# Chunk attention feeding a mixture of experts on one core: softmax held in PSUM, attention of later token pairs at fixed places

## The chip, the cores and the metric

The kernel runs on one core of a Trainium2 chip. The metric is the device time in microseconds (us) of one execution; the time before is the median of three runs. Five engines work side by side, each through its own list of instructions in order: TensorE (PE) multiplies, VectorE (DVE) and ScalarE (ACT) read and write PSUM and SBUF, GpSimd (POOL) works in SBUF, and SyncE (SP) issues the DMAs.

## The reference

Inputs are q, k, v of shape 8 x 8 x 576 x 64 (batch, heads, sequence, head size), four expert probabilities for each of 4608 tokens, and two weight matrices for each of four experts.

```
scores = q_c @ k_c^T / 8            # in chunks of 64 positions, nothing across chunks
attn   = exp(scores - max(scores))
attn   = attn / (sum(attn) + 1e-9)
x      = attn @ v_c                 # then (4608 tokens, 512)
p      = probs / (sum(probs) + 1e-9)
out    = sum over e of  p[:, e] * (relu(x @ w1[e]) @ w2[e])     # 512 -> 1024 -> 512
```

## The kernel before

**Stages.** The 4608 tokens are nine blocks of 512: one block by itself, and then four pairs of blocks. Each expert's hidden size of 1024 is cut in two, so there are eight passes over weights for each stage: passes 0 to 7 for the single block (`startup`, `plain_pass`), passes 8 to 15 for pair 0 (`first_pair_pass`), and passes 16 to 39 for pairs 1, 2 and 3 (`later_pass`, eight passes each). A pair is multiplied by a scheme of seven products in place of eight, over 2 x 2 blocks of weights (a11 to a22, sums s1 to s4) and tokens or hidden values (b11 to b22, sums t1 to t4).

**Two halves of a number.** An fp32 operand is split into a rounded "hi" part, which ScalarE casts, and the remainder "lo", which VectorE or GpSimd makes by subtraction. Each product is then three matmuls (`TERMS`, L455), issued at L461.

**Units of the later passes.** In a later pass the first matrix's units are called g1 to g7 and h1 to h7 (`LaterGroup`, two halves of the rows), and the second matrix's units of the pass before are a1 to a7 and b1 to b7 (`Outer`). A unit is six matmuls. `WOVEN` is the written order of the 28 units; a "place" below is an index into it:

```
0 a1  1 g1  2 a2  3 g2  4 g6  5 a5  6 g5  7 a6  8 a3  9 g7  10 a7  11 g4  12 g3  13 a4
14 h1 15 h2 16 b1 17 b5 18 h6 19 b6 20 b3 21 h5 22 b7 23 h7 24 b2 25 b4  26 h4  27 h3
```

After the unit at each place come the functions listed in `at` for it. What g and h leave in PSUM is copied (L523), added (L662), cut at zero and scaled (L628) by ScalarE and VectorE into hidden values; their sums are at L634, their hi casts at L640 and their lo parts on GpSimd at L643. What a and b leave is added to the output sums by VectorE (L689). The banks are named: g and h use A0, B0, C0, and a and b use A1, B1, C1, so a unit waits until VectorE or ScalarE has read what the unit before left in its bank. Pass 16 has no a or b units, as no pass of this kind lies before it, and runs g and h alone in the same order.

**Attention.** A tile is 128 tokens; eight tiles make a pair. A tile has five steps (`STEPS`): scores (PE into the PSUM tile "psa" of two banks), softmax (VectorE maximum L148 and subtraction L149, ScalarE exponential L153), weights (VectorE sum L197, plus 1e-9 L202, reciprocal L203, multiplication L204), transpose (PE L163 and ScalarE L165) and values (PE L172 and ScalarE L179). The generator `attention` yields between steps, and `Beside.go` takes steps at a rate: in passes 17 to 22 of a pair (and 25 to 30 of the next) it is called at the eight places of `ASIDE` (1, 4, 8, 11, 15, 18, 22, 25), with 40 steps spread over 42 calls. The tiles of the first block have functions of their own in `startup` (L186 to L204 by way of `less_max`, `a_exp`, `a_norm`).

**Weights and the ring.** During passes 8 to 15 the split weights are written to DRAM. Later passes read them back in units of 512 KB through six SBUF buffers: three for the first matrix (ring 0) and three for the second (ring 1), refilled by `ring_next` when both halves of a unit are used. All these DMAs go through SyncE's list.

Of the kernel before, what the change touches and what calls it, by code (L numbers as in the profile page):

```python
# [30 lines left out]
def chunk_attention_moe(ctx: ExitStack, tc: tile.TileContext, qk, v, v0, dp, w1, w2, out):  # L31
# [110 lines left out]

    def a_softmax(t):

        s = st[t]
        e = s["e"] = att.tile([P, HG, 2, C], F32, name="e")
        m = small.tile([P, 2, HG], F32, name="m")
        nc.vector.tensor_reduce(out=m, in_=s["sc"], op=ALU.max, axis=AX)  # L148
        nc.vector.tensor_tensor(  # L149
            out=e.rearrange("p j c k -> p c j k"), in0=s["sc"],  # L150
            in1=m.unsqueeze(3).broadcast_to([P, 2, HG, C]), op=ALU.subtract,
        )
# [29 lines left out]

    def less_max(a, src):
        n = a.shape[1]
        m = small.tile([P, n], F32, name=f"m{n}")
        nc.vector.tensor_reduce(out=m, in_=src, op=ALU.max, axis=AX)  # L186
        nc.vector.tensor_tensor(
            out=a, in0=src, in1=m.unsqueeze(2).broadcast_to([P, n, C]), op=ALU.subtract
        )

    def a_exp(a):
        nc.scalar.activation(out=a, in_=a, func=AF.Exp, scale=1.0 / C**0.5)

    def a_norm(e):
        n = e.shape[1]
        z = small.tile([P, n], F32, name=f"z{n}")
        nc.vector.tensor_reduce(out=z, in_=e, op=ALU.add, axis=AX)  # L197
        a_scale(e, z)

    def a_scale(e, z):  # L200
        n = e.shape[1]
        nc.vector.tensor_scalar_add(z, z, 1e-9)  # L202
        nc.vector.reciprocal(out=z, in_=z)  # L203
        nc.vector.tensor_tensor(  # L204
            out=e, in0=e, in1=z.unsqueeze(2).broadcast_to([P, n, C]), op=ALU.mult
        )

# [649 lines left out]
    nc.vector.memset(zeros, 0.0)  # L857
    idle = ps_a.tile([P, SUB], F32, name="psa")

    def keep_warm(n, cols=SUB):  # L860

        for _ in range(n):
            nc.tensor.matmul(
                idle[:, :cols], lhsT=zeros[:, :P], rhs=zeros[:, :cols], start=True, stop=True
            )
# [12 lines left out]

    def start_e(t):
        return att.tile([P, 2 * HG, C], F32, name=("e", "pt")[t % 2])  # L880

    def subtract_max(t):
        es[t] = start_e(t)
        less_max(es[t], sc[t])

    def startup(beside):
# [21 lines left out]
        start_x(1)  # L908
        subtract_max(2)
        a_exp(es[2])  # L910
        w_load(1, 0, 1, 0)
# [4 lines left out]
        plain_hidden(0, first, order=RHS_LO_LAST)  # L916
        a_norm(es[2])
        w2_split(0, 1)
        plain_hidden(1, first, order=RHS_LO_LAST)
        subtract_max(3)  # L920
        a_exp(es[3])
        w2_split(1, 0)
        plain_hidden(2, first, order=RHS_LO_LAST)
        start_transpose(2)
        a_norm(es[3])
        w2_split(1, 1)
# [55 lines left out]
    def plain_pass(n, beside, x, ahead_of=None):  # L982
# [32 lines left out]
        add(at, 4, lambda: w[0].hi("a12"), lambda: x.hi("b21"), lambda: w[0].hi("s1"))  # L1015
        add(at, 4, lambda: w[0].lo("a12"), lambda: x.lo("b21"), lambda: w[0].lo("s1"))
        add(at, 5, lambda: w[0].sum3(), lambda: w[0].sum4(), ahead_of.load)
        add(at, 6, lambda: w[0].hi("s3"), lambda: w[0].lo("s3"))
        add(at, 6, lambda: w[0].hi("a22"), lambda: w[0].lo("a22"))
        add(at, 6, lambda: w[0].hi("s4"), lambda: w[0].lo("s4"))  # L1020
# [4 lines left out]
    def first_pair_pass(n, held, made, beside, ahead_of):  # L1025

# [19 lines left out]
        begin_w2 = 5 if n == n_pass else 0  # L1046
        if begin_w2 == 0:
            add(at, 0, w2.sum1, w2.sum2)
# [43 lines left out]
        add(at, 13, lambda: x.lo("t1"), lambda: x.hi("t3"))  # L1092
        add(at, 14, lambda: x.lo("t3"))
        add(at, 16, lambda: x.hi("b22"))
        add(at, 17, lambda: x.lo("b22"))
        add(at, 17, lambda: [ring_load(i, r) for r in range(3) for i in range(2)])
        add(at, 18, x.sum2, lambda: x.hi("t2"))
        add(at, 19, lambda: probs_load(n + 1, 0), lambda: probs_load(n + 1, 1))
        add(at, 19, lambda: x.lo("t2"))
        add(at, 20, x.sum4, lambda: x.hi("t4"))  # L1100
        add(at, 20, ahead_of.load)
        add(at, 21, lambda: x.lo("t4", nc.gpsimd))
        issue(steps, at, beside)
# [24 lines left out]
    def later_pass(n, ahead, late, beside, ahead_of):  # L1128

# [3 lines left out]
        left, sc = Units(n), Scaled(n)  # L1133
        steps = {f"gh"[g]: LaterGroup(g, left, sc, False) for g in range(2)}
        if ahead:
            steps |= {"ab"[g]: Outer(g, n - 1, ahead[1], ahead[0], False) for g in range(2)}

# [3 lines left out]
        for i, f in late:  # L1141
            add(at, i, f)
        if ahead:
            second_half(at, ahead[0])

# [22 lines left out]
        if last_pass and more:  # L1168
# [11 lines left out]
            late = [  # L1180
                (0, lambda: x.hi("b22")), (0, ahead_of.load),
                (7, lambda: x.lo("t4", nc.gpsimd)), (7, lambda: x.lo("b22", nc.gpsimd)),
            ]
        for i, name in enumerate(WOVEN):
            if name[0] in steps:
                getattr(steps[name[0]], f"p{name[1]}")()
# [62 lines left out]
    with tc.manual_schedule():  # L1249
        beside = [Beside(0, (n_pass - 3) * 2 * NK), Beside(1, (n_pass - 1) * 26 - 4)]  # L1250
        beside += [Beside(pair, (n_pass - 3) * len(ASIDE) + 2) for pair in range(2, n_pairs + 1)]
        startup(beside[0])
        x = None
        for n in range(1, n_pass):
            if n == n_pass - 2:
                x = Tokens(0)
            held, made = plain_pass(n, beside[0], x, beside[1] if n == n_pass - 1 else None)
        for n in range(n_pass, 2 * n_pass):
            held, made = first_pair_pass(n, held, made, beside[1], beside[2])
        ahead, late = None, []  # L1260
        for n in range(2 * n_pass, n_run):
            pair = n // n_pass - 1
            ahead, late = later_pass(
                n, ahead, late, beside[1 + pair], beside[min(2 + pair, n_pairs)]
            )
        last_products(ahead)
# [45 lines left out]
```

## Time and profile before

| | us |
|---|---|
| median of three runs (1585.38 to 1593.53) | 1587.99 |
| profiled execution | 1587.58 |
| its span, first to last instruction | 1585.8 |
| PE busy in the span | 1531.3 |
| DVE busy | 924.8 |
| POOL busy | 888.0 |
| ACT busy | 574.9 |

The profiled execution's time is 1.8 us more than its span, and 0.4 us less than the median. "Idle" before an instruction is the time in which its engine had nothing running; the name behind the arrow is what ended it, by engine, tile and line. A row of stages gives the stage's limits and length, then for each engine its busy time and its count of instructions, and then the granted TensorE clock (1.00 is full), the DMA share and GB/s.

### The profile page before, as it was taken

What the parts mean: (1) busy time and instruction counts of PE and PEld (TensorE: products, weight loads), DVE (VectorE), ACT (ScalarE), POOL (GpSimd) and SP (SyncE); (2) the same over time, 40 slices, a digit from 0 to 9 for tenths busy, and PEclk for the clock granted to TensorE, in tenths of its full rate; (3) what the DMA queues carried; (4) which work ended last, traced back from release to release, by engine and by line L of the source; (5) the groups of instructions that cost most, each with busy time, mean ns of one, the idle gap of its engine ahead of it and who ended that gap; (6) DMA issues with size and microseconds to landing.
All of it is one profiled execution on the core that took longest, in us unless ns stands there. A gap on an engine that the chain in (4) does not pass through costs nothing.

```text
span 1585.8 us, 23406 instructions
## 1 busy us (share of the span) xinstructions
PE 1531.3 (97%) x8854; PEld 1238.8 (78%) x8854; DVE 924.8 (58%) x1287; ACT 574.9 (36%) x999; POOL 888.0 (56%) x665
## 2 busy tenths in 40 slices
PE   7999999999999999999999999998999999999998
PEld 5878877888888777787777777786877788888886
DVE  5444554444444555766767855666667755566665
ACT  3343443344444424332333434232333443323332
POOL 2343576677766525545555665444455755555654
PEclk9999999999999999999999999999999999999999
DMA  5344347877666575656655667565655576666664
GB/s 188 120 124 138 107 165 251 297 249 237 231 226 225 200 249 173 212 187 209 201 194 184 196 211 236 182 226 174 203 191 191 179 232 207 194 204 195 203 193 138
DMA packets 164831, 314.16 MB, mean 198 GB/s; under 512 B 14176, under 2 KB 79984, under 8 KB 164720
## 3 DMA queue, kind: packets, MB, share of 16 engines
q1 hardware_dynamic: 164720, 312.68, 60.6%
q8 instruction: 70, 1.15, 0.3%
q14 instruction: 41, 0.34, 0.1%
HBM read 244.39 MB, written 68.23 MB: 197 GB/s over the span
## 4 chain that ended last, share of the span: by engine, by line
PE 80%; DVE 9%; POOL 5%; ACT 2%; DMA 1%; issue 1%; SPq 0%; DVEq 0%; ACTq 0%; POOLq 0%
PE A L461 39%; PE C L461 23%; PE B L461 14%; POOL hfl L643 2%; DVE acc L689 1%; DVE wraw L634 1%; PE psa L172 1%; DVE e L204 1%; PE psa L138 1%; PE psa L163 1%; DVE z L202 1%; POOL wf L279 1%; DVE xl L279 1%; POOL hfl L279 1%; DVE z L197 1%
## 5 line engine op out<-in xcount | busy, mean ns | idle before, releaser
L643 POOL TENSOR_TENSOR hfl<-wraw,hfh 128x512 fp32r<-128x512 f32 x288 | 388.1, 1367 | 219.7 <-ACT hfh L640 196.5
L461 PE MATMUL A<-xh,wf 128*128 128x512 f32 (+1 forms) x1112 | 384.8, 392 | 11.2 <-DVE wraw L628 9.5
L461 PE MATMUL A<-hfh,wf 128*128 128x512 f32 x768 | 272.2, 396 | 10.2 <-DVE acc L689 10.2
L461 PEld LDWEIGHTS A<-xh,wf 128*128 128x128 f32 x1112 | 207.9, 188 | 59.4 <-DVE wraw L628 12.2
L523 ACT COPY s<-A 128x512 f32<-128x512 f32 x192 | 112.6, 587 | 385.7 <-PE A L461 385.1
L640 ACT CAST hfh<-wraw 128x512 fp32r<-128x512 f32 x288 | 172.3, 622 | 203.7 <-POOL wraw L634 61.0
L461 PE MATMUL A<-xl,wf 128*128 128x512 f32 (+1 forms) x556 | 215.2, 388 | 0.0
L461 PE MATMUL C<-xh,wf 128*128 128x512 f32 (+1 forms) x584 | 201.0, 391 | 1.7 <-DVE B L662 1.7
L461 PEld LDWEIGHTS A<-hfh,wf 128*128 128x128 f32 x768 | 145.1, 189 | 44.0 <-DVE acc L689 13.4
L689 DVE TENSOR_TENSOR acc<-A,acc 128x512 f32<-128x512 f32 x174 | 119.4, 686 | 99.7 <-PE A L461 99.4
L461 PE MATMUL A<-hfl,wf 128*128 128x512 f32 x384 | 150.7, 393 | 0.0
L461 PE MATMUL C<-hfh,wf 128*128 128x512 f32 x384 | 134.7, 392 | 0.2
L279 POOL TENSOR_TENSOR hfl<-wraw,hfh 128x512 fp32r<-128x512 f32 x64 | 87.2, 1388 | 84.0 <-ACT hfh L276 79.0
L634 POOL TENSOR_TENSOR wf<-wraw,wf 128x512 f32<-128x512 f32 x24 | 31.1, 1296 | 177.6 <-DVE wf L628 177.6
L461 PEld LDWEIGHTS C<-xh,wf 128*128 128x128 f32 x584 | 109.2, 188 | 24.9 <-DVE B L662 2.2
L461 PE MATMUL B<-xh,wf 128*128 128x512 f32 (+1 forms) x384 | 126.9, 384 | 1.3 <-DVE acc L757 1.3
L279 POOL TENSOR_TENSOR wf<-wraw,wf 128x512 fp32r<-128x512 f32 x70 | 93.5, 1358 | 56.8 <-ACT wf L276 56.6
L461 PEld LDWEIGHTS A<-xl,wf 128*128 128x128 f32 x556 | 104.4, 188 | 20.4 <-POOL xl L279 0.6
L461 PE MATMUL C<-xl,wf 128*128 128x512 f32 (+1 forms) x292 | 113.0, 389 | 1.4 <-POOL xl L279 1.4
L689 DVE TENSOR_TENSOR acc<-C,acc 128x512 f32<-128x512 f32 x90 | 62.0, 689 | 66.3 <-PE C L461 65.7
L643 POOL TENSOR_TENSOR hfl<-wf,hfh 128x512 fp32r<-128x512 f32 x48 | 72.6, 1512 | 44.1 <-ACT hfh L640 43.8
L461 PEld LDWEIGHTS C<-hfh,wf 128*128 128x128 f32 x384 | 72.1, 188 | 16.2 <-DVE acc L689 1.1
(177 smaller groups left out, 2738.2 us busy)
## 6 DMA issues: line engine op xcount, KB each, us to landing
wf<-w SPq DMA_DIRECT2D x336, 512.0 KB, 4.0
wraw<-in_w SPq DMA_DIRECT2D x128, 256.0 KB, 3.7
w<-wf SPq DMA_DIRECT2D x112, 256.0 KB, 4.3
qk_in<-in_qk SPq DMA_DIRECT2D x32, 512.0 KB, 4.5
v_in<-in_v SPq DMA_DIRECT2D x32, 256.0 KB, 4.0
w<-hfl SPq DMA_DIRECT2D x32, 256.0 KB, 2.4
w<-hfh SPq DMA_DIRECT2D x32, 256.0 KB, 2.6
w<-hfh SPq DMA_DIRECT2D x48, 128.0 KB, 2.7
```

Of the source, the lines that this page charges most:

```text
L138: nc.tensor.matmul(s["sc"][half, c, j], lhsT=s["x"][rows, g, 0, h], rhs=s["x"][rows, g, 1, h], start=True, stop=True,)
L163: nc.tensor.transpose(ps[:, j], s["e"][:, j].rearrange("p c k -> p (c k)"), ident)
L172: nc.tensor.matmul(av[half, c, j], lhsT=s["v"][rows, 2 * j + odd], rhs=s["pt"][rows, j, half], start=True, stop=True,)
L197: nc.vector.tensor_reduce(out=z, in_=e, op=ALU.add, axis=AX)
L202: nc.vector.tensor_scalar_add(z, z, 1e-9)
L279: eng.tensor_tensor(out=t[1], in0=src, in1=t[0].bitcast(F32), op=ALU.subtract)
L461: nc.tensor.matmul(out, lhsT=lhs(k, a), rhs=rhs(k, b), start=first and i == 0, stop=last and i == len(parts) - 1, skip_group_check=not (fi ...
L523: nc.scalar.copy(out=t, in_=self.a)
L634: (eng or nc.vector).tensor_tensor(out=self.values[place, k], in0=self.values[a, k], in1=self.values[b, k], op=op)
L640: nc.scalar.copy(out=self.part(name, 0)[:, k], in_=self.values[name, k])
L643: (eng or nc.gpsimd).tensor_tensor(out=self.part(name, 1)[:, k], in0=self.values[name, k], in1=self.part(name, 0)[:, k].bitcast(F32), op=A ...
L689: nc.vector.tensor_tensor(out=acc[key], in0=src, in1=acc[key], op=ALU.add)
```

## The change

- **Softmax.** Maximum, subtraction and exponential now work in place in PSUM; the sum of the exponentials and its addition of 1e-9 lie in an unused part of the same PSUM tile (in `startup`, of the tile that keeps PE warm, which becomes two banks). The reciprocal goes to SBUF, and the last multiplication reads PSUM and writes the weights `e` to SBUF. `e` is allocated at the weights step, not at the softmax step; "psa" is held until then.
- **Startup order.** The weights of tile 0 come ahead of the softmax of tile 1.
- **Attention of pairs 2 and 3.** In later passes the rate is gone. `TILES` says which tile is worked on in which pass, at the places `EARLY` (4, 6, 9, 11) or `LATE` (13, 17, 21, 24): scores, softmax and the next loads at the first place, weights at the second, transpose at the third, values at the fourth.
- **Pass 16** has a function and an order of its own, in which g and h are mixed and have separate banks (A0, B0, C0 and A1, B1, C1); its ring loads are at first all for ring 0.
- **First tiles of pair 1.** In pass 15 the hi and lo parts of the tokens come later, one pair of them at a place; in passes 7 and 8 the parts of the weight blocks a22, s3 and s4 change place.
- **In later passes** the sum t4 of the first half goes on GpSimd behind b21's lo part, one place later.

```diff
     def a_scores(t):
         s = st[t]
-        s["sc"] = halves(ps_a.tile([P, 2, 2 * HG * C], F32, name="psa"))
+        s["psa"] = ps_a.tile([P, 2, 2 * HG * C], F32, name="psa")
+        s["sc"] = halves(s["psa"])
...
     def a_softmax(t):
+        less_max(st[t]["sc"])
+        a_exp(st[t]["sc"])
+
+    def a_weights(t):
         s = st[t]
-        e = s["e"] = att.tile([P, HG, 2, C], F32, name="e")
-        m = small.tile([P, 2, HG], F32, name="m")
-        nc.vector.tensor_reduce(out=m, in_=s["sc"], op=ALU.max, axis=AX)
-        nc.vector.tensor_tensor(
-            out=e.rearrange("p j c k -> p c j k"), in0=s["sc"],
-            in1=m.unsqueeze(3).broadcast_to([P, 2, HG, C]), op=ALU.subtract,
-        )
-        nc.scalar.activation(out=e, in_=e, func=AF.Exp, scale=1.0 / C**0.5)
-
-    def a_weights(t):
-        e = st[t]["e"].rearrange("p j c k -> p (j c) k")
-        a_norm(e)
+        s["e"] = att.tile([P, HG, 2, C], F32, name="e")
+        z = s["psa"][:, 0, HG * C : HG * C + 2 * HG].rearrange("p (c j) -> p c j", c=2)
+        a_norm(s["e"].rearrange("p j c k -> p c j k"), s["sc"], z)
...
+    def less_max(a):
+        m = small.tile(a.shape[:-1], F32, name=f"m{len(a.shape)}")
+        nc.vector.tensor_reduce(out=m, in_=a, op=ALU.max, axis=AX)
+        m = m.unsqueeze(len(a.shape) - 1).broadcast_to(a.shape)
+        nc.vector.tensor_tensor(out=a, in0=a, in1=m, op=ALU.subtract)
...
+    def a_norm(e, a, z):
+        nc.vector.tensor_reduce(out=z, in_=a, op=ALU.add, axis=AX)
         nc.vector.tensor_scalar_add(z, z, 1e-9)
+        r = small.tile(a.shape[:-1], F32, name=f"z{len(a.shape)}")
+        nc.vector.reciprocal(out=r, in_=z)
+        r = r.unsqueeze(len(a.shape) - 1).broadcast_to(a.shape)
+        nc.vector.tensor_tensor(out=e, in0=a, in1=r, op=ALU.mult)
...
     def ring_next(i, r):
         last = n_ring - N_SLOT
-        if r + 3 < n_ring and (i == 0 or r < last):
+        if i == 0 and 3 <= r < 6:
+            ring_load(1, r - 3)
+        elif i == 0 and r < 3:
+            ring_load(0, r + 6)
+        elif i == 0 and r + 3 < n_ring or r < last:
             ring_load(i, r + 3)
...
     def startup(beside):
...
-        subtract_max(0)
-        a_exp(es[0])
-        subtract_max(1)
-        a_exp(es[1])
+        start_softmax(0)
+        start_weights(0)
+        start_softmax(1)
         for f, k in QUADS[:3]:
             w1_split(f, k, nc.gpsimd)
-        a_norm(es[0])
         start_transpose(0)
         w1_split(1, 1, nc.gpsimd)
-        a_norm(es[1])
+        start_weights(1)
...
-        add(at, 8, lambda: x.hi("b11"))
-        add(at, 9, lambda: x.lo("b11"), lambda: x.hi("b21"))
-        add(at, 10, lambda: x.lo("b21"))
-        add(at, 12, lambda: x.hi("t1"))
...
-        add(at, 17, lambda: [ring_load(i, r) for r in range(3) for i in range(2)])
...
+        for i, name in zip((13, 14, 16, 17, 19), ("b11", "b21", "t1", "t3", "b22")):
+            add(at, i - 1, lambda name=name: x.hi(name))
+            add(at, i, lambda name=name: x.lo(name))
+        add(at, 17, lambda: [ring_load(0, r, (RINGS[0] + RINGS[1])[r]) for r in range(6)])
...
-    ASIDE = (1, 4, 8, 11, 15, 18, 22, 25)
+    EARLY, LATE = (4, 6, 9, 11), (13, 17, 21, 24)
+    TILES = {
+        1: ((LATE, 0),), 2: ((EARLY, 1),), 3: ((EARLY, 2), (LATE, 3)), 4: ((EARLY, 4),),
+        5: ((EARLY, 5), (LATE, 6)), 6: ((EARLY, 7),),
+    }
...
+    def attend(at, pair, places, i):
+        t = (1 + pair * PAIR) * NT + i
+        add(at, places[0], lambda: a_scores(t), lambda: a_softmax(t), lambda: a_load_v(t))
+        if i + 1 < PAIR * NT:
+            add(at, places[0], lambda: a_load(t + 1))
+        for place, step in zip(places[1:], STEPS[2:]):
+            add(at, place, lambda step=step: step(t))
+
+    FIRST = "g1 g2 g6 g5 h1 g7 h2 h6 g4 g3 h5 h7 h4 h3".split()
+
+    def first_later_pass(n, *_):
+        at = {}
+        left, sc = Units(n), Scaled(n)
+        steps = {"gh"[g]: LaterGroup(g, left, sc, True) for g in range(2)}
...
+        for i, name in enumerate(FIRST):
+            getattr(steps[name[0]], f"p{name[1]}")()
+            for f in at.get(i, ()):
+                f()
+        return (sc, left), []
...
     def later_pass(n, ahead, late):
...
-        add(at, 25, lambda: sc.sum("t4", 0, nc.gpsimd))
         put(26, "b21", 1)
+        add(at, 26, lambda: sc.sum("t4", 0, nc.gpsimd))
...
+        if pair + 1 < n_pairs:
+            for places, i in TILES.get(n % n_pass, ()):
+                attend(at, pair + 1, places, i)
...
-            if i in ASIDE and not first_pass and not last_pass and (n % n_pass > 1 or i > 16):
-                beside.go()
```

More of the change, by code (lines that the diff above doesn't have):

```diff
@@ L857, in chunk_attention_moe @@
     nc.vector.memset(zeros, 0.0)
-    idle = ps_a.tile([P, SUB], F32, name="psa")
+    idle = ps_a.tile([P, 2, SUB], F32, name="psa")
     def keep_warm(n, cols=SUB):
@@ L863, in keep_warm @@
             nc.tensor.matmul(
-                idle[:, :cols], lhsT=zeros[:, :P], rhs=zeros[:, :cols], start=True, stop=True
+                idle[:, 0, :cols], lhsT=zeros[:, :P], rhs=zeros[:, :cols], start=True, stop=True
             )
@@ L877, in load_all, with start_softmax, start_weights @@
         w_load(1, 0, 0, 1)
[L879 to L884, printed above, removed]
+    def start_softmax(t):
+        less_max(sc[t])
+        a_exp(sc[t])
+    def start_weights(t):
+        es[t] = att.tile([P, 2 * HG, C], F32, name=("e", "pt")[t % 2])
+        a_norm(es[t], sc[t], idle[:, 1, t * 2 * HG : (t + 1) * 2 * HG])
     def startup(beside):
@@ L1023, in plain_pass, with first_pair_pass @@
         return steps[-1], w[0]
-    def first_pair_pass(n, held, made, beside, ahead_of):
+    def first_pair_pass(n, held, made, beside):
         last_pass = n % n_pass == n_pass - 1
@@ L1046, in first_pair_pass @@
         begin_w2 = 5 if n == n_pass else 0
[L1047 removed]
+        if begin_w2:
+            for name in ("s3", "s4"):
+                add(at, 0, lambda name=name: made.hi(name), lambda name=name: made.lo(name))
+        else:
             add(at, 0, w2.sum1, w2.sum2)
@@ L1124, in chunk_attention_moe, with first_load, put, later_pass @@
     )
-    ASIDE = (1, 4, 8, 11, 15, 18, 22, 25)
-    ALONE = "a1 b1 a2 a5 b5 a6 b6 a3 b3 a7 b7 b2 a4 b4".split()
-    def later_pass(n, ahead, late, beside, ahead_of):
+    EARLY, LATE = (4, 6, 9, 11), (13, 17, 21, 24)
[3 more added lines that the diff above has]
+    }
+    ALONE = "a1 b1 a2 a5 b5 a6 b6 a3 b3 a7 b7 b2 a4 b4".split()
+    def first_load(pair):
+        if pair < n_pairs:
+            a_load((1 + pair * PAIR) * NT)
+    def attend(at, pair, places, i):
[10 more added lines that the diff above has]
+        steps = {"gh"[g]: LaterGroup(g, left, sc, True) for g in range(2)}
+        def put(i, name, k):
+            add(at, i, lambda: sc.hi(name, k), lambda: sc.lo(name, k))
+        put(2, "b11", 0)
+        put(6, "b22", 0)
+        put(7, "b11", 1)
+        put(9, "b21", 0)
+        add(at, 9, lambda: sc.sum("t3", 0), lambda: sc.sum("t2", 0))
+        put(10, "t2", 0)
+        add(at, 11, lambda: sc.sum("t1", 0))
+        put(12, "b22", 1)
+        put(12, "t1", 0)
+        add(at, 12, lambda: sc.sum("t4", 0, nc.gpsimd))
+        put(13, "b21", 1)
+        put(13, "t3", 0)
+        add(at, 13, lambda: sc.sum("t1", 1), lambda: sc.sum("t3", 1))
+        for i, name in enumerate(FIRST):
[3 more added lines that the diff above has]
+        return (sc, left), []
+    def later_pass(n, ahead, late):
         first_pass, last_pass = n % n_pass == 0, n % n_pass == n_pass - 1
@@ L1133, in later_pass @@
         left, sc = Units(n), Scaled(n)
-        steps = {f"gh"[g]: LaterGroup(g, left, sc, False) for g in range(2)}
-        if ahead:
-            steps |= {"ab"[g]: Outer(g, n - 1, ahead[1], ahead[0], False) for g in range(2)}
+        steps = {"gh"[g]: LaterGroup(g, left, sc, False) for g in range(2)}
+        steps |= {"ab"[g]: Outer(g, n - 1, ahead[1], ahead[0], False) for g in range(2)}
         def put(i, name, k, of=sc):
@@ L1258, in chunk_attention_moe @@
         for n in range(n_pass, 2 * n_pass):
-            held, made = first_pair_pass(n, held, made, beside[1], beside[2])
+            held, made = first_pair_pass(n, held, made, beside[1])
         ahead, late = None, []
         for n in range(2 * n_pass, n_run):
[L1262 to L1265, printed above, removed]
+            ahead, late = (later_pass if n > 2 * n_pass else first_later_pass)(n, ahead, late)
         last_products(ahead)
```

55 lines of the change are left out of this document (13 added, 42 removed).

## The prediction

> **What bounds the kernel.** First the page's head (the profiled execution took 1587.58 us, 1.8 more than its span), then the span cut by stages, to see where PE has nothing to run. The stage rows give limits, length, then PE, PEld, DVE, ACT and POOL busy time with counts, granted clock, DMA share, GB/s.
>
> ```profile
> span 1585.8 us, 23406 instructions
> ```
>
> ```profile
> 0.00:34.00 34.00, 23.57 (x311) 17.97 (x312) 20.02 (x36) 13.04 (x24) 11.54 (x14) 0.97 0.67 219
> 222.00:573.00 351.00, 346.70 (x1989) 281.59 (x1990) 166.45 (x235) 146.89 (x259) 230.58 (x180) 1.00 0.74 250
> 573.00:605.00 32.00, 26.76 (x113) 20.51 (x112) 17.94 (x22) 11.41 (x20) 17.12 (x13) 1.00 0.39 129
> 605.00:880.00 275.00, 263.52 (x1616) 212.18 (x1615) 179.62 (x255) 89.21 (x155) 142.96 (x108) 0.99 0.62 200
> 880.00:920.00 40.00, 37.67 (x160) 29.13 (x159) 30.74 (x39) 18.30 (x28) 31.01 (x19) 1.00 0.61 193
> 950.00:1225.00 275.00, 263.51 (x1621) 212.17 (x1620) 178.21 (x254) 90.67 (x158) 141.45 (x107) 0.99 0.62 202
> 1225.00:1265.00 40.00, 37.67 (x160) 29.15 (x159) 30.98 (x39) 18.30 (x28) 31.25 (x19) 1.00 0.58 186
> 1265.00:1560.00 295.00, 295.00 (x1319) 244.19 (x1317) 176.27 (x245) 98.63 (x170) 171.38 (x131) 1.00 0.64 203
> ```
>
> PE is the bound: in 1265 to 1560, passes with no attention, it is never idle, and 295 us over 1319 matmuls are 0.224 us each, so a unit of six takes 1.34. The change removes no PE work, so all it can win is PE idle time. The two stretches with attention of pairs 2 and 3 lose 275.00 - 263.52 = 11.48 and 11.49 us. Pass 16 (573 to 605) loses 5.24, the two pair changes (880 to 920, 1225 to 1265) 2.33 each, passes 8 to 15 lose 4.30.
>
> Next, who ends the idle time in 605 to 880 (total, times, longest), and the clock just after two of its stalls:
>
> ```profile
> PE A L461 <- DVE wraw L628: 4.7, 2, 2.4
> PE A L461 <- DVE acc L689: 4.6, 2, 2.3
> PE psa L163 <- DVE e L204: 2.2, 2, 1.2
> 673.80:677.20 3.40, 3.40 (x10) 2.72 (x11) 1.15 (x2) 0.38 (x1) 0.45 (x1) 0.50 0.00 0
> 1107.30:1110.70 3.40, 3.40 (x11) 2.71 (x11) 1.32 (x3) 0.62 (x1) 0.28 (x2) 0.50 0.00 0
> ```
>
> All of it is VectorE arriving late, in six stalls per pair. After two of the eight long ones (over both pairs) the granted clock is 0.50 for 3.4 us, which costs another 1.7 us of PE work each.
>
> One of each long kind, in the timeline (start, length, instruction, idle before it):
>
> ```profile
> 725.90 0.68 DVE L197 TENSOR_REDUCE z<-e 128x8 f32<-128x512 f32 x1
> 726.61 1.14 DVE L202 TENSOR_SCALAR z<-z 128x8 f32<-128x8 f32 x1
> 728.02 1.47 DVE L204 TENSOR_TENSOR e<-e,z 128x512 f32<-128x512 f32 x1
> 729.41 0.68 DVE L628 SCALAR_TENSOR_TENSOR wraw<-A,s 128x512 f32<-128x512 f32 x1
> 730.15 0.50 PE L461 MATMUL A<-xh,wf 128*128 128x512 f32 x1 [2.39 <-DVE wraw L628]
> ```
>
> The weights of a tile were issued at place 25, between b4 and h4. VectorE spends 725.90 to 729.41 on them and only then reads h4's bank A0, for which the next pass's g1 waits 2.39 us.
>
> ```profile
> 666.76 1.13 ACT L640 CAST hfh<-wraw 128x512 fp32r<-128x512 f32 x2
> 667.44 2.54 POOL L643 TENSOR_TENSOR hfl<-wraw,hfh 128x512 fp32r<-128x512 f32 x2 [5.28 <-DVE acc L689]
> 668.77 1.76 DVE L634 TENSOR_TENSOR wraw<-wf,wraw 128x512 f32<-128x512 f32 x1 [1.39 <-POOL hfl L643]
> 673.05 0.68 DVE L689 TENSOR_TENSOR acc<-A,acc 128x512 f32<-128x512 f32 x1
> 673.78 0.80 PE L461 MATMUL A<-hfh,wf 128*128 128x512 f32 x1 [2.29 <-DVE acc L689]
> ```
>
> Here the softmax had been issued at place 15. Its exponential stood in ScalarE's list ahead of b11's casts (666.76), GpSimd's lo parts came late, the sum t2 (668.77) waited 1.39 us for them, the weights at place 18 stood behind that sum, and b6's output addition (673.05) behind the weights. Unit b7 (673.78) needs b6's bank. The third kind is a transpose issued too soon after its weights.
>
> **The change, part by part.** *Softmax in PSUM.* The rows of its instructions (minimum/median/maximum ns):
>
> ```profile
> L204 DVE TENSOR_TENSOR e<-e,z x34: 691/1476/1709, 11.8 to 1190.0; 128x512 f32<-128x512 f32 x34
> L202 DVE TENSOR_SCALAR z<-z x36: 171/468/1276, 11.4 to 1188.5; 128x8 f32<-128x8 f32 x36
> L149 DVE TENSOR_TENSOR e<-psa,m x32: 691/691/694, 53.7 to 1182.3; 128x512 f32<-128x512 f32 x32
> L148 DVE TENSOR_REDUCE m<-psa x32: 680/681/686, 53.0 to 1181.6; 128x8 f32<-128x512 f32 x32
> L197 DVE TENSOR_REDUCE z<-e x34: 674/676/679, 10.7 to 1187.8; 128x8 f32<-128x512 f32 x34
> ```
>
> The multiplication with both operands in SBUF takes 1476 in the median; the subtraction of the same shape, with its large operand in PSUM, never over 694. The new multiplication is of that second form, so I take 0.69 (ends 0.69 and 1.48). The addition on z moves to PSUM, where no row shows it: between 0.17 and 0.47, and I take 0.2, as its long cases look like the multiplication's. The reciprocal keeps some 0.2, what the timeline leaves between 727.75 and 728.02. Weights then cost 0.68 + 0.2 + 0.2 + 0.69 = 1.8 us against 0.68 + 0.47 + 0.2 + 1.48 = 2.8 in the median. That alone gives PE nothing; it shortens the stalls. Maximum and subtraction stay, and the exponential only changes its memory, hidden beside matmuls. "psa" is held longer, but its next user is the same tile's transpose, which waits for the weights anyway.
>
> [...]
>
> *Fixed places.* Weights come at place 6 or 17 and never behind b4, so the 2.4 us stalls at g1 go. The late softmax is at 13, and its weights at 17 come ahead of t2 (place 18), not behind it; the exponential no longer stands before b11's casts. Transposes follow weights by three or four units, 4.0 us or more, against 1.8 us of work. What is late next? For an early tile, the weights can begin about 2.2 us after the scores (0.68 + 0.69 + the exponential's 0.63 and the hand-overs), and two units last 2.7; behind them waits a6's addition, whose bank is wanted three units later: nothing lost. For a late tile, b5's addition ends near 667.4 in the example, the weights 669.2, t2 by 669.9 to 671.0, b6's addition by 670.6 to 671.7, and PE would be ready for b7 at 671.3: 0 to 0.4 us lost, for six late tiles 0 to 2.4. I take 1.0. Gain: 11.48 + 11.49 + 2 x 1.7 - 1.0 = **25.4 us**.
>
> *Pass 16.* The waits in 573 to 605:
>
> ```profile
> PE B L461 <- POOL hfl L643: 2.0, 1, 2.0
> PE C L461 <- DVE B L662: 1.7, 1, 1.7
> PE A L461 <- ACT s L523: 1.5, 2, 0.7
> ```
>
> Mixing g and h removes the copy wait between g7 and g4. But h6's copy goes to the tile "s2" that g3's addition, two units later, still has to read; ScalarE stands until then, casts and the copy of h7 queue behind it, and VectorE's sums for t2 with them. I work this out as about 0.2 at h7, 1.9 at h4, and 1.1 at pass 17's a2, whose last lo part is fourth in GpSimd's list: 3.2 against 5.24. Gain **2.0** (0 to 5.2). The six first ring loads are the same number of bytes; nothing waits for them before.
>
> *First tiles reordered.* In passes 8 to 15 the largest stall stands behind these:
>
> ```profile
> PE C L461 <- DVE hfl L469: 2.4, 4, 1.6
> 544.89 2.33 DVE L279 TENSOR_TENSOR xl<-xraw,xh 128x1024 fp32r<-128x1024 f32 x1
> 547.74 1.71 DVE L279 TENSOR_TENSOR xl<-xraw,xh 128x1024 fp32r<-128x1024 f32 x1
> ```
>
> The two lo parts of b11 and b21 sit between g3's result and the reading of its bank. They move four places later, behind that reading. Gain **1.6** (0 to 2.4). They are hidden behind the four whole output tiles (12 matmuls, 2.7 us each) that end pass 15; without these the last one, t4's, would be late by its own length, about 2.3 us. The moves in passes 7 and 8 I put at nothing, hidden behind matmuls; the 2.7 us left in this stage bound them.
>
> *t4 behind b21.* At each pair change GpSimd is busy 31 of 40 us, so its b21 part comes one operation earlier, but its later parts end when they did. Gain **1.0** of the 4.66 (0 to 1.9).
>
> *Startup.*
>
> ```profile
> 10.79 0.63 ACT L192 ACTIVATE pt<-pt 128x512 f32<-128x512 f32 x1 [1.88 <-DVE pt L187]
> 11.33 1.64 ACT L276 CAST wf<-wraw 128x512 fp32r<-128x512 f32 x3
> 13.33 0.59 ACT L836 COPY s<-B 128x512 f32<-128x512 f32 x1 [0.36 <-PE B L832]
> 29.23 1.15 PE L845 MATMUL A<-s,ws 64*64 64x64 f32 x32 [1.45 <-ACT s L836]
> 31.34 0.69 DVE L204 TENSOR_TENSOR pt<-pt,z 128x512 f32<-128x512 f32 x1
> ```
>
> Tile 1's maximum and subtraction now stand behind tile 0's weights, so its exponential (10.79) slips by about 1.6, the three casts with it, and the copy of tile 0's transpose (13.33) to 14.6: 1.25 us late, into the first hidden product. The cheaper weights win most of it back (tile 3's end at 31.4 in place of 32.0). But tile 2's values (29.23) go to the bank where tile 3's scores lie, now held until tile 3's weights end, so their 1.15 us move behind it. Loss **0.8** (-0.6 to 1.6).
>
> Sum: -25.4 - 2.0 - 1.6 - 1.0 + 0.8 = -29.2 us, so 1587.58 - 29.2 = 1558.4 for the profiled execution. That one stood 0.4 below the median of 1587.99; I forecast **1558.5**.
>
> **Rivals.** *Half of it stays.* If the b7 stalls come from GpSimd's lateness and not from the order, the four of 2.3 us and the two half-clock stretches stay: 9.2 + 3.4 = 12.6, time 1571. For it: the 1.39 us wait in the row at 668.77. Against it: 1265 to 1560 has the same sums and no idle.
>
> *The idle time only changes place.* If PE is ahead of VectorE or GpSimd by as much at the new places, the 23 us come back: about 1584. Against it: VectorE is busy 179.62 of 275 us there, POOL 142.96; neither is full.
>
> *Slower.* At place 4 or 13 the exponential is issued only one or two units before other ScalarE work and its weights two units later. If ScalarE stands at the exponential long enough that each of the 16 tiles meets one 2.3 us stall (a6's or b6's addition late), that is 36.8 us plus the clock halved for one in four, 4 x 1.7 = 6.8, against 30.2 saved: 1601. It decides from 1.9 us per tile on. The slack reckoned above speaks against it.
>
> *More than that.* Pass 16, the pair changes and startup at their good ends, no late-tile loss: 25.4 + 1.0 + 5.2 + 2.4 + 1.9 + 0.6 = 36.5, so 1551.
>
> **How the numbers follow.** Forecast 0.62, with its own range 1553 to 1565 from the ends of the small terms; half stays 0.20; changes place 0.07; slower 0.06; more 0.05. The range 1550 to 1575 holds the first two and the last, 0.87. What can be told from no change here is 0.5%, 8 us: faster 0.87, same 0.07, slower 0.06.
>
> **What would show it.** Right: between 605 and 1225 no PE wait on L628 or L689 over 0.5 us, no clock of 0.50 there, the final multiplication near 0.69 in all tiles; no wait at 550; pass 16 still losing about 3 us, at h4 and at a2. Wrong: new waits of about 2 us at a7, b7 or a transpose once per tile, or startup's first output product more than 1.6 us late.

## The result, and the profile after

The changed kernel takes **1561.48 us** in the median of four runs (1560.53 to 1562.57), against 1588.52 for the kernel before (the three runs behind 1587.99 and a fourth, 1585.38 to 1593.53): a ratio of 0.9827, 95% interval 0.98 to 0.9854. Its profiled execution took 1560.53 us. Its page's head:

```profile
span 1558.7 us, 23407 instructions
PE 1527.6 (98%) x8854; PEld 1240.8 (80%) x8854; DVE 918.0 (59%) x1288; ACT 574.3 (37%) x999; POOL 883.2 (57%) x664
```

The span is 27.1 us shorter, with the same 8854 matmuls. Where this came from can be read from the first matmul of a pass, since PE does the same work between two of them. PE's timeline, at the first matmul of pass 8, 16, 24, 32 and of the last products; first the kernel before, then after:

```profile
219.60 0.47 PE L461 MATMUL A<-xh,wf 128*128 128x512 f32 x1
573.36 0.39 PE L461 MATMUL A<-xh,wf 128*128 128x512 f32 x1
899.55 0.50 PE L461 MATMUL A<-hfh,wf 128*128 128x512 f32 x1 [0.53 <-DVE acc L689]
1244.79 0.50 PE L461 MATMUL A<-hfh,wf 128*128 128x512 f32 x1 [0.53 <-DVE acc L689]
1556.15 0.39 PE L461 MATMUL A<-hfh,wf 128*128 128x512 f32 x1
```

```profile
222.69 0.47 PE L455 MATMUL A<-xh,wf 128*128 128x512 f32 x1
574.52 0.39 PE L455 MATMUL A<-xh,wf 128*128 128x512 f32 x1
885.17 0.50 PE L455 MATMUL A<-hfh,wf 128*128 128x512 f32 x1 [0.53 <-DVE acc L683]
1217.16 0.50 PE L455 MATMUL A<-hfh,wf 128*128 128x512 f32 x1 [0.48 <-DVE acc L683]
1528.57 0.39 PE L455 MATMUL A<-hfh,wf 128*128 128x512 f32 x1
```

| stretch | before | after | moved by | forecast |
|---|---|---|---|---|
| start to pass 8 | 219.60 | 222.69 | +3.09 | +0.8 |
| passes 8 to 15 | 353.76 | 351.83 | -1.93 | -1.6 |
| passes 16 to 23 | 326.19 | 310.65 | -15.54 | -14.7 |
| passes 24 to 31 | 345.24 | 331.99 | -13.25 | -13.2 |
| passes 32 to 39 | 311.36 | 311.41 | +0.05 | -0.5 |
| rest of the span | 29.65 | 30.13 | +0.48 | 0 |

The forecast for passes 16 to 23 is half of the 25.4 us for the fixed places, and 2.0 for pass 16; for 24 to 31 the other half, and half of t4's 1.0. The sum of the moves is -27.1, that of the forecast -29.2.

The stages of the changed kernel, in the columns of the rows before (limits, length, PE, PEld, DVE, ACT, POOL, clock, DMA share, GB/s):

```profile
576.00:608.00 32.00, 29.94 (x124) 23.96 (x123) 19.24 (x23) 13.02 (x23) 19.33 (x14) 0.95 0.52 164
608.00:850.00 242.00, 242.00 (x1535) 196.61 (x1534) 164.18 (x236) 84.74 (x147) 131.00 (x101) 1.00 0.65 209
850.00:906.00 56.00, 51.85 (x222) 40.77 (x221) 44.32 (x57) 21.26 (x33) 40.20 (x24) 1.00 0.61 201
940.00:1182.00 242.00, 242.00 (x1539) 196.71 (x1538) 163.84 (x236) 85.67 (x149) 129.65 (x99) 1.00 0.66 211
1182.00:1238.00 56.00, 52.19 (x223) 40.98 (x222) 44.32 (x57) 21.23 (x33) 40.13 (x24) 1.00 0.61 193
```

In 608 to 850 and 940 to 1182, where the attention of pairs 2 and 3 runs, PE is never idle: all twelve stalls are gone, and no clock of 0.50 is left there. But 850 to 906 and its twin 1182 to 1238 lose 4.15 and 3.81 us, where the kernel before loses 2.33 at the pair change. The waits of the kernel before in 880 to 920, and of the changed kernel in 850 to 906:

```profile
PE B L461 <- POOL hfl L643: 0.9, 1, 0.9
PE C L461 <- POOL xl L279: 0.7, 1, 0.7
PE A L461 <- DVE acc L689: 0.5, 1, 0.5
```

```profile
PE C L455 <- DVE acc L683: 1.6, 1, 1.6
PE A L455 <- POOL xl L268: 1.2, 1, 1.2
PE C L455 <- POOL xl L268: 0.7, 1, 0.7
PE A L455 <- DVE acc L683: 0.5, 1, 0.5
```

The first two of the changed kernel are new. The wait of 1.6 is at a3 of pass 23, the last pass of the pair, that of 1.2 at g4 of pass 24, and both have their like at the next pair change (1.3 and 1.1). The wait of 0.9 before, at a2 of pass 24, is gone.

The softmax's instructions (ns, minimum/median/maximum) came out as taken:

```profile
L195 DVE TENSOR_TENSOR e<-psa,z x32: 690/691/692, 61.3 to 1147.0; 128x512 f32<-128x512 f32 x32
L191 DVE TENSOR_SCALAR psa<-psa x36: 173/174/175, 11.9 to 1146.6; 128x8 f32<-128x8 f32 x36
```

The addition's 174 ns in PSUM stand beside a least of 171 in SBUF, and the sum's 690 from PSUM (median) beside 676 from SBUF: 3 and 14 ns more.

### The profile page after: what moved, and what is told of

Same layout as the page of the kernel before. It is cut to its first block, busy times and chain, and to the rows that moved or that the text cites. A ratio compares the mean times of both kernels' runs of the same rounds, so it can differ in the third digit from the quotient of the medians.

```text
span 1558.7 us, 23407 instructions
## 1 busy us (share of the span) xinstructions
PE 1527.6 (98%) x8854; PEld 1240.8 (80%) x8854; DVE 918.0 (59%) x1288; ACT 574.3 (37%) x999; POOL 883.2 (57%) x664
## 4 chain that ended last, share of the span: by engine, by line
PE 87%; DVE 4%; POOL 4%; DMA 3%; ACT 2%; issue 1%; SPq 0%; DVEq 0%; ACTq 0%; POOLq 0%
PE A L455 42%; PE C L455 25%; PE B L455 15%; PE psa L168 1%; PE psa L139 1%; POOL hfl L637 1%; PE psa L159 1%; DVE xl L268 1%; DMA w<-hfh 1%; DMA w<-wf 1%; POOL wf L268 1%; DMA wraw<-in_w 1%; DVE acc L683 1%; POOL xl L268 1%; PE psa L769 1%
## 5 line engine op out<-in xcount | busy, mean ns | idle before, releaser
L683 DVE TENSOR_TENSOR acc<-A,acc 128x512 f32<-128x512 f32 x174 | 119.3, 685 | 79.6 <-PE A L455 78.6
L683 DVE TENSOR_TENSOR acc<-C,acc 128x512 f32<-128x512 f32 x90 | 62.0, 690 | 58.9 <-PE C L455 54.6
```

Source lines behind the costliest of these rows:

```text
L683: nc.vector.tensor_tensor(out=acc[key], in0=src, in1=acc[key], op=ALU.add)
```

## The experiments

All are edits of one of the two kernels; in the diffs "..." marks what is left out. Where a pass is said to begin at a time, that is its first matmul in PE's timeline. Traces of the same code differ by one or two us among themselves (startup of the kernel before: the first output product at 32.85 and, in the run of softmax alone, at 33.86; the changed kernel: pass 16 at 574.52 and, timed again, at 575.58). A stretch of half clock (1.6 us in pass 16 below) or a single wait (1.2 us at g1 of pass 24) comes in some of them and not in others. So a time from one run is weak evidence below that.

**Softmax in PSUM alone, and fixed places alone.** The first takes the kernel before and gives only the tiles of pairs 0 to 3 their new softmax. The second takes the changed kernel, with all its other parts, and gives these tiles their old softmax.

```diff
# psum_only: the kernel before
     def a_softmax(t):
+        in_place_max(st[t]["sc"])
+        a_exp(st[t]["sc"])
+
+    def a_weights(t):
...
-        e = s["e"] = att.tile([P, HG, 2, C], F32, name="e")
...
+        psum_norm(s["e"].rearrange("p j c k -> p c j k"), s["sc"], z)
# places_only: the changed kernel, the same exchange the other way round
```

`in_place_max` and `psum_norm` are what the changed kernel calls `less_max` and `a_norm`.

> The kernel before, with only the softmax of the tiles of pairs 0 to 3 kept in PSUM; startup, the rate of the attention steps, pass 16 and the first tiles are as before. Theory (the order in VectorE's list makes the stalls, their length is set by the weights): the multiplication falls to 0.69 us and the addition to 0.2, so the four stalls at g1 (2.39) lose about 1.75 each, the four at b7 (2.29) about 0.8, the four at the transpose nearly all; some 9 of the 23 us stay and the clock is not halved there: about 1571. Rival (only the places matter): 20 us or more of the 23 stay, about 1584.

> The changed kernel, but with the softmax of the tiles of pairs 0 to 3 in SBUF as before (startup's tiles stay in PSUM). Theory: at the new places the 2.8 us of weights have room too, at most 0.8 us more is lost at b7 for each of six late tiles: 1561 to 1566. Rival (the fixed places only work because the weights are short): a stall of 1 us or more for each of 14 tiles in pairs 2 and 3, above 1573.

Measured: softmax alone 1571.09 us (ratio to the kernel before 0.9897, interval 0.9873 to 0.992); places alone 1561.64 (0.984, 0.9822 to 0.9858). The waits of softmax alone in 605 to 880, and of places alone its stages with attention:

```profile
PE A L471 <- DVE acc L699: 3.0, 2, 1.5
PE A L471 <- DVE wraw L638: 1.3, 2, 0.6
```

```profile
608.00:850.00 242.00, 242.00 (x1535) 196.74 (x1535) 164.49 (x235) 85.01 (x148) 132.10 (x101) 1.00 0.66 210
942.00:1184.00 242.00, 242.00 (x1539) 196.78 (x1538) 165.59 (x236) 85.99 (x149) 130.53 (x99) 1.00 0.67 211
```

With softmax alone the stalls at b7 and g1 keep their places and lose what VectorE saves in them, 2.3 to 1.5 and 2.4 to 0.6; those at the transpose go, and the clock behind the eight that stay is 1.00. With the places alone every one of them is gone, although the multiplication takes up to 1.82 us again. So the two parts are two ways to the same gain and do not add: either the weights get short, or they get a place where their length does not matter. The second reaches further: on top of it the short weights show no gain, 0.984 against the changed kernel's 0.9827. Both rivals fall.

**Late tiles' weights at place 25.** The place of the old stall at g1, with the short weights.

```diff
-    EARLY, LATE = (4, 6, 9, 11), (13, 17, 21, 24)
+    EARLY, LATE = (4, 6, 9, 11), (13, 25, 26, 27)
```

> The changed kernel with LATE = (13, 25, 26, 27): the weights of six tiles come at place 25, between b4 and h4, as in the stall of the kernel before. Theory: h4's bank is read 1.8 us late, so g1 waits 0.5 to 0.8 us (2.39 less the 1.75 that PSUM saves), and the transpose at 26 waits about 0.7 for its weights: 1.0 to 1.6 us a tile, 6 to 10 us in all, about 1569. Rival (with short weights the place does not matter): under 1 us in all, 1561 to 1562.

Measured: 1567.76 us in one run. The waits in 605 to 880:

```profile
PE psa L159 <- DVE e L195: 3.2, 3, 1.3
```

Beside these only the 1.6 at a3 is left, which the changed kernel has too. The place matters: 6 us in all, as the theory said. But of the two waits it added up, only one is there. The transposes at 26 take all of it (0.5 to 1.3 each), and g1 does not wait. It would not wait without them either: at the tile with the longest wait, VectorE has read h4's bank at 720.82, and g1 comes at 724.43. With softmax alone the weights at place 25 begin 0.9 us after h4 ends (725.67), here 0.7 before it ends (718.36). The softmax now stands at 13, no longer a few places ahead of the weights; that this is the reason was not tested.

**t4 back at place 25.** In the changed kernel GpSimd's sum t4 comes behind b21's lo part.

```diff
+        add(at, 25, lambda: sc.sum("t4", 0, nc.gpsimd))
         put(26, "b21", 1)
-        add(at, 26, lambda: sc.sum("t4", 0, nc.gpsimd))
```

> The changed kernel with the GpSimd sum t4 back at place 25, ahead of b21's lo part. Theory: the waits that the changed kernel newly has in the last pass of pairs 1 and 2 (1.61 and 1.34 us at a3, behind VectorE's sums that take 1.7 us beside GpSimd in place of 0.69) come from t4's new place; they go below 0.5, and a2 in passes 17, 24 and 32 waits about 0.9 to 2.0 again. Rival (VectorE's list of token differences makes them): the two waits stay above 1 us.

Measured: 1557.18 in one run. The new waits at a3 fall from 1.6 and 1.3 us to 0.1. The new ones at g4 go too, and a2 in passes 24 and 32 waits 0.9 for GpSimd again, as in the kernel before. In the timeline of VectorE and GpSimd around pass 23's start, first the changed kernel, then this one:

```profile
845.42 1.29 POOL L628 TENSOR_TENSOR wraw<-wraw 128x512 f32<-128x512 f32 x1
845.56 1.70 DVE L628 TENSOR_TENSOR wraw<-wf,wraw 128x512 f32<-128x512 f32 x1
848.34 5.22 POOL L637 TENSOR_TENSOR hfl<-wraw,hfh 128x512 fp32r<-128x512 f32 x3 [1.63 <-ACT hfh L634]
848.50 1.68 DVE L628 TENSOR_TENSOR wraw<-wraw 128x512 f32<-128x512 f32 x1
855.82 0.68 DVE L683 TENSOR_TENSOR acc<-C,acc 128x512 f32<-128x512 f32 x1
856.55 0.50 PE L455 MATMUL C<-hfh,wf 128*128 128x512 f32 x1 [1.61 <-DVE acc L683]
```

```profile
843.69 1.29 POOL L628 TENSOR_TENSOR wraw<-wraw 128x512 f32<-128x512 f32 x1
844.95 1.28 POOL L637 TENSOR_TENSOR hfl<-wraw,hfh 128x512 fp32r<-128x512 f32 x1
845.58 1.21 DVE L628 TENSOR_TENSOR wraw<-wf,wraw 128x512 f32<-128x512 f32 x1
848.03 0.68 DVE L628 TENSOR_TENSOR wraw<-wraw 128x512 f32<-128x512 f32 x1
854.36 0.68 DVE L683 TENSOR_TENSOR acc<-C,acc 128x512 f32<-128x512 f32 x1
```

VectorE's sums have both operands in SBUF. Two of them, 1.21 and 0.68 us with t4 early, take 1.70 and 1.68 with t4 late. With t4 late GpSimd has begun an instruction 0.14 and 0.16 us before each; with t4 early it has begun one 0.63 us before the first and none before the second. The addition that frees a3's bank comes 1.46 us later (855.82 against 854.36), about what the two sums lose together. The traces of the next two runs show the same sums at 1.69 and 1.68, and at 1.19 and 0.68. So one move of one GpSimd instruction by one place did that. At g4 the account is another: GpSimd's lo parts for pass 24 come as far behind the pass's start in both (14.6 and 14.5 us), and PE, no longer held at a2, is there earlier and waits. Timed beside the changed kernel on one chip:

> The changed kernel once more, on the chip of the next three, as their yardstick: 1560 to 1563.

> The changed kernel with t4 back at place 25, timed. Theory (its two waits of 1.6 and 1.3 us and what hangs on them are the cost of that one move): 2 to 4 us below the changed kernel. Rival (the single time of 1557.18 was the spread of the runs): within 1 us of it.

Measured: the changed kernel 1561.70 us (1560.58 to 1563.04; ratio 0.9831, interval 0.9814 to 0.9848), t4 at place 25 1557.86 (1557.63 to 1558.7; 0.9807, 0.9791 to 0.9824). The ranges do not meet, and the medians are 3.8 us apart. Of this, 1.6 stands ahead of pass 16 in the two traces (575.58 against 574.00), where the kernels are the same. From pass 16 to the end t4's move costs 2.3 us in these two traces, and 3.3 in the two of the single run and the changed kernel above. So its cost is 2 to 4 us, as the theory had it.

**Startup: order and table load.**

```diff
# start_order
         start_softmax(0)
-        start_weights(0)
         start_softmax(1)
         for f, k in QUADS[:3]:
             w1_split(f, k, nc.gpsimd)
+        start_weights(0)
# early_table
     def startup(beside):
+        warm = small.tile([P, 2], F32, name="warm")
+        nc.vector.memset(warm, 0.0)
+        a_exp(warm)
         load_all()
```

> The changed kernel with startup's old order: softmax of tiles 0 and 1, the three weight splits, then the weights of tile 0. Theory: tile 1's exponential and the casts behind it no longer wait for tile 0's weights, so the copy of tile 0's transpose, at 16.50 us in the changed kernel, comes about 2.6 us earlier, and pass 1 begins at about 53 us in place of 55.8 (half-clock stretches can move this by 1.7): total about 1558.5. Rival (startup is set by the bank that tile 2's values wait for, not by this order): pass 1 begins within 1 us of 55.8.

> The changed kernel with one small exponential (128x2) on zeros as ScalarE's first instruction. Theory: the table load, which in the changed kernel starts only when tile 0's subtraction ends (9.18 us, 1.28 long), then runs in the first 3 us as in the kernel before, and all of startup comes 1.2 us earlier: pass 1 at about 54.5. Rival (the load is hidden elsewhere): pass 1 within 0.4 us of 55.8.

Measured, in one run each: old order 1559.34 us, early table 1560.8. Pass 1 begins at 52.2 and 55.1, against 55.8 in the changed kernel and 52.9 in the one before. The changed kernel's startup in the timeline, from the table load to the first output product:

```profile
9.18 1.28 ACT L187 ACT_TABLE_LOAD   x1 [9.18 <-DVE A L184]
14.46 0.58 ACT L187 ACTIVATE A<-A 128x512 f32<-128x512 f32 x1 [3.40 <-DVE A L184]
16.50 0.59 ACT L830 COPY s<-B 128x512 f32<-128x512 f32 x1
33.98 1.98 PE L839 MATMUL A<-s,ws 64*64 64x64 f32 x32 [3.21 <-issue]
36.66 0.78 PE L455 MATMUL B<-hfh,hfh 128*128 128x512 f32 x1
```

The load and the first output product in the kernel before:

```profile
0.73 1.28 ACT L192 ACT_TABLE_LOAD   x1 [0.73 <-PEq L1302]
32.85 0.78 PE L461 MATMUL B<-hfh,hfh 128*128 128x512 f32 x1
```

The copy of tile 0's transpose comes at 16.50; with the old order it comes at 12.86, with the early table at 15.68. The old order shows the larger effect, 3.6 us at the copy and 3.6 at pass 1; both theories hold in sign, the table load's with 0.6 at pass 1 in place of the 1.3 expected. The totals of these single runs, one 1.2 us below the changed kernel's range and one within it, carry little weight. And the clock takes part: PE's wait of 3.1 us before tile 0's values has a stretch of 6.8 us at 0.50 around it in the changed kernel, and with the old order that one is gone while another stands later. First the changed kernel, then the old order:

```profile
13.40:20.20 6.80, 3.73 (x42) 2.88 (x42) 3.13 (x7) 3.74 (x8) 4.56 (x4) 0.50 0.72 245
33.90:37.30 3.40, 3.31 (x38) 3.13 (x39) 1.00 (x3) 0.79 (x2) 0.08 (x1) 0.50 0.46 150
```

```profile
13.40:20.20 6.80, 6.45 (x145) 5.94 (x146) 3.11 (x5) 2.55 (x6) 2.79 (x3) 1.00 0.88 287
28.50:35.30 6.80, 6.27 (x45) 5.41 (x46) 2.52 (x7) 1.17 (x2) 0.52 (x1) 0.50 0.25 77
```

That the first stretch goes cannot be put down to the order alone: in the runs `best` and `start_t4` below, which have the old order and the early load together, the clock is 0.50 and 0.55 in 13.4 to 16.8. There the copy comes at 12.96 and 13.77, and pass 1 at 53.55 and 54.55. So the old order brings the copy 2.7 to 3.6 us earlier, and pass 1 between 1.2 and 3.6.

**Pass 16: a buffer of its own for h6's copy.**

```diff
     class LaterGroup(Group):
+        def keep(self, name):
+            if not (self.apart and self.g and name == "s2"):
+                return super().keep(name)
+            t = att.tile([P, SUB], F32, name="pt")
+            nc.scalar.copy(out=t, in_=self.a)
+            return t
...
-            self.h = h
+            self.h, self.apart = h, apart
```

> The changed kernel; in pass 16 the copy that h6 leaves goes to a buffer of its own and not to s2. Theory: the copy no longer waits for g3's addition, ScalarE's list flows, and h4's wait of 1.95 us falls to the 0.73 of one copy or less; the half-clock stretch behind it may go (1.7). Pass 16, 23.3 us long, takes 20.0 to 22.2; up to 1.5 us of it comes back as a wait of pass 17's a2 for GpSimd. Total 1557 to 1560. Rival (GpSimd sets the end of pass 16, whatever ScalarE does): pass 16 shorter, but pass 24 begins within 0.5 us of 885.2.

Measured: 1562.02 us in one run, above the 1557 to 1560 expected. Pass 16 takes 20.8 us, not 23.3. But 1.6 of this difference is the half clock behind h4, which this trace does not have: in the trace of t4 timed again, also without it, pass 16 takes 21.7. Pass 24 begins 0.7 us earlier (884.48), and pass 32 no earlier (1217.57 against 1217.16), since g1 of pass 24 now waits 1.2, as it does in some runs of either t4 place and not in others. The waits in 570 to 606:

```profile
PE B L455 <- POOL hfl L637: 1.5, 1, 1.5
PE A L455 <- ACT s L517: 1.5, 1, 1.5
```

h4's wait falls by 0.5 only. ScalarE's timeline shows why:

```profile
591.56 0.62 ACT L634 CAST hfh<-wraw 128x512 fp32r<-128x512 f32 x1 [2.94 <-DVE wraw L628]
592.09 0.58 ACT L517 COPY s<-A 128x512 f32<-128x512 f32 x1
```

The cast of t2 waits 2.94 us for VectorE's sum and stands ahead of h7's copy (592.09), which h4 needs. That sum starts as far into the pass as in the changed kernel, 16.06 us; what is shorter is the sum itself, 0.69 us against 1.60, and GpSimd's lo parts no longer begin 0.3 us ahead of it (590.29 and 590.58 in the changed kernel). What PE wins is met at pass 17's a2, where it now waits 1.5 us for GpSimd. The rival, that GpSimd sets the end of pass 16, is nearer to it, though pass 24 begins a little more than the 0.5 us earlier that it allows.

**Several edits together.** First t4, both startup edits and h6's buffer; then without h6's buffer; then that one with another bank for the values of startup's tile 2.

```diff
# start_t4_bank, beside the t4 and startup edits above
         plain_hidden(3, first, order=RHS_LO_LAST)
+        turn[0] += 1
         start_values(2)
```

> The changed kernel with four edits together: t4 at place 25, startup's old order, the early table load, h6's own buffer. Theory (their gains lie in different stretches and add): 1557.2 of t4 alone, less 3 to 4 in startup, less 1 to 2.5 in pass 16: 1551 to 1553. Rival (PE reaches the same later waits of GpSimd and VectorE earlier, and waits there longer): 1555 or more.

> The changed kernel with t4 at place 25, startup's old order and the early table load, without h6's own buffer. Theory: startup's gain of 2 to 3.5 us stays, and without the own buffer pass 17 does not meet GpSimd's wait of 1.5 us earlier: 1553.5 to 1556. Rival (later waits take up what startup wins): 1556.5 or more, like the four edits together.

> As the one before, and tile 2's values take the next bank of the row, not the one that holds tile 3's scores. Theory (tile 2's values wait for tile 3's weights only because of the bank): their 3.2 us wait falls to about 1.3, and pass 1 begins 1 to 2 us earlier, with one half-clock stretch less at best 1.7 more; all later banks of the first block shift by one, which may move the 1.3 us wait at pass 8. Total 1552 to 1555. Rival (the values wait for something else): the wait stays over 3 us.

Measured: four edits 1556.97 us (1555.64 to 1558.59; ratio 0.98, interval 0.9781 to 0.982); without h6's buffer 1555.42 (1554.76 to 1558.6; 0.9795, 0.9777 to 0.9813); with the other bank 1555.11 (1552.84 to 1555.69; 0.9786, 0.9768 to 0.9803). The gains of the four edits do not add: 1551 to 1553 was expected, and as the rival has it PE waits later for GpSimd and VectorE, in this trace 1.5 us at pass 17's a2 and 1.2 at g1 of passes 24 and 32. h6's buffer shows no gain beside the others. With the other bank the 3.2 us wait of tile 2's values is gone from the list; its startup waits for ScalarE are

```profile
PE B L839 <- ACT s L830: 2.1, 2, 1.4
```

with 1.4 before the values of tile 2, and the first output product comes at 31.65, not at 34.16 (that trace is of its kernel's slowest run, 1558.6). In the median the bank brings 0.3 us, which these runs cannot tell from nothing. The last two kernels beat both given ones; the last is 6.6 us below the changed kernel, timed on the same chip.

## Why the prediction was right, and where not

The forecast was 1558.5, the result 1561.5, inside the range of the forecast itself (1553 to 1565).

- **The main term held.** 25.4 us were forecast for the fixed places; passes 16 to 31 moved by 28.8 against 27.9 forecast with the smaller terms. The stall readings held one by one: softmax alone left 1.5 and 0.6 us where the working of its parts gives 2.29 - 0.8 and 2.39 - 1.75. But that the sums agree so well is in part luck, as errors cancelled. By an estimate from the rows of the kernel before, a stall costs more than its idle time: idle counts from the end that the profile gives a matmul, 0.39 us after its start, where matmuls without idle time begin 0.22 apart (295 us over 1319 in 1265 to 1560), and the first matmul behind a stall is 0.33 ahead of the second (730.15 and 730.48), another 0.1. That makes 0.27 more for a stall, 3 us for twelve of them. And the late tiles lost nothing at b7, where I took 1.0. Against them stood the new waits of 1.6 and 1.3 at a3, and t4's missing gain.
- **The rivals.** That half of the stalls stay, or that VectorE comes late at the new places, once per tile or as much in all, is ruled out by the two rows without idle time. At the pair changes idle time did only change its place, from a2 to g4.
- **Its own signs.** The multiplication at 0.690 to 0.692, no clock of 0.50 between 605 and 1225, no wait at 550 and the wait at h4 came as named. Two did not: PE waits 1.6 us on L683 (L689 before) at a3, within 605 to 1225, and startup's first output product is 3.8 us late, which was named as a sign of being wrong.
- **What PSUM brings.** "That alone gives PE nothing; it shortens the stalls" was right as far as it went: alone it takes 15.5 us off by the stalls (1586.61 to 1571.09, timed together), and at the fixed places it adds nothing that the times tell. The prediction did not say that the places would do without it.
- **Startup failed, in two steps.** A loss of 0.8 was forecast, 1.6 at the worst; the table has 3.09. The slip of tile 1's exponential was put at 1.6 us; it was 3.7 (10.79 to 14.46). 1.3 of this is the table load, which was missed altogether: at 0.73 us in the kernel before, behind the subtraction at 9.18 after. Some 0.8 more is this execution's own, as its first scores began that much later (6.42 against 5.64). And "the cheaper weights win most of it back" was wrong: tile 3's weights end at 33.9, not at the 31.4 of the working, and the first output product came 3.8 us later (36.66 against 32.85). The step on the bank of tile 2's values held: with another bank their wait falls from 3.2 to 1.4. How much of the 3.09 belongs to the change stays open, as the trace before is a favourable one: with the same startup, in the run of softmax alone, the first output product comes at 33.86 and pass 8 at 221.73. With the changed startup pass 8 begins between 222.41 and 224.02 in seven traces.
- **t4 failed in sign.** A gain of 1.0 was forecast, with 0 as the worse end; undoing the move wins 2 to 4. It failed in two steps. The wait at a2 went as forecast, but that GpSimd's later parts "end when they did" was no comfort: PE now waits 1.2 and 1.1 for them at g4, so nothing was gained. And the step reckoned only with GpSimd's own list, and not with VectorE's sums beside it, although it had the rows of 1476 against 691 ns in hand: they make the waits at a3.
- **Pass 16: the number held, the cause in part.** Waits of 0.2 at h7, 1.9 at h4 and 1.1 at a2 were worked out. Measured were 0.1, 1.95, and at a2 1.5 in executions without a half-clock stretch behind h4, 0 in the changed kernel's, which has one. Of the cause, a buffer in place of s2 takes away 0.5 of h4's wait; the rest, by the timeline, stands behind t2's cast.
- **First tiles held:** 1.93 against 1.6, and the wait at 550 is gone.

## What to carry to other kernels

When an engine that is half idle stalls the busy one, look at what stands ahead of the awaited instruction in its list before making anything faster: here a better place removed all of what a shorter instruction removed in part. After such a move look for the neighbours: an instruction moved by one place on GpSimd slowed two on VectorE (1.21 and 0.68 us to 1.70 and 1.68) and cost about a tenth of the whole gain. And check what an engine does once only, such as a table load (1.28 us here), whenever the first instruction of its kind gets a new wait.

## What the runs showed of the hardware

- **Half a clock that cost nothing.** In the changed kernel the 1.95 us wait in pass 16 is followed by 3.4 us at a clock of 0.50; in the run with t4 timed again the same wait is not. The clock rows behind that wait, changed kernel and t4 again:

```profile
593.70:597.00 3.30, 3.30 (x9) 2.61 (x8) 2.32 (x4) 1.41 (x3) 2.34 (x3) 0.50 0.20 77
```

```profile
592.90:596.20 3.30, 3.30 (x15) 2.71 (x16) 2.81 (x5) 1.92 (x4) 2.35 (x2) 1.00 0.22 82
```

  Nine matmuls in one, 15 in the other. Yet with t4 early the way from pass 16 to pass 24 took 309.18 us in the execution with the slow stretch and 309.38 in the one without: the second waits 1.5 us for GpSimd at a2 instead. So a wait of 1.95 us was followed by a halved clock in one execution and not in another; what decides it these runs do not show.
- **The table load's place.** It ran at 0.73 us in the kernel before, and in the changed one at 9.18, behind the subtraction that its exponential waits for. A first exponential on zeros brings it back to 0.73. Why it was placed so is not settled by these runs.
- **One sum, slow and fast, beside GpSimd.** The same 128x512 sum on VectorE, both operands in SBUF, took 1.68 us where a GpSimd instruction had begun 0.16 us before it, and 0.68 where one began 0.34 us after it (848.37 in the run with t4 early). In pass 31 of the changed kernel it took 1.40, 0.44 us behind such a beginning (1180.72 and 1180.28).
